# K's 32-point product of a long convolution: 64 by 64 quarters of the array in place of 128-row products

## The chip, the cores and the metric

The kernel runs on one core of one Trainium2 chip. The metric is the device time of one execution in microseconds, as the median of several runs.

## The reference

The block is a conditioned residual layer with two branches over 2048 positions and 576 channels:

```python
mod = (_silu(c) @ w_mod).reshape(c.shape[0], 6, 1, -1)
sa, ca, ga, sb, cb, gb = ...
h = _layernorm(x) * (1 + ca) + sa
x = x + ga * _A_ref(h, ...)      # state-space layer as a long convolution
h = _layernorm(x) * (1 + cb) + sb
x = x + gb * _B_ref(h, ...)      # gMLP with a 2048 x 2048 spatial product
```

In the first branch each channel d has a kernel of 2048 points, made of 128 complex poles, and is convolved with it:

```python
P = jnp.exp(logdA[:, :, None] * l[None, None, :])
K = jnp.einsum("dn,dnl,dn->dl", Cc, P, dB).real
y = irfft(rfft(up) * rfft(Kp))[..., :L] + u * Dskip
```

## The kernel before

The convolution is done by transforms written as matrix products, and the work of this document lies in its first part, where K is made and transformed. A point l of K is split into 32 steps of 64, l = 64 a + b. The 576 channels are taken in 36 groups of 16. For one group g, these functions run in order (lines of the profile):

- `e_unit` (L440 to 452) makes exponents on TensorE, into a tile of two PSUM banks (`ps2`, tile "ps") and one of a single bank (`ps1`, tile "pk"), and ScalarE takes the exponential.
- `t_unit` (L456 to 483) makes phases on TensorE into a "ps" tile. ScalarE (L480) and VectorE (L481) both read it.
- `s_unit` (L485 to 488) takes sine and cosine on ScalarE, `p_unit` (L490 to 502) multiplies on VectorE.
- `kg_unit` (L504 to 514) sums over the 128 poles: fp32 products with 32 columns of weights, four of them side by side in the array, into a "pk" tile. ScalarE copies it to the tile `kab`, whose 128 partitions are four channels by 32 points a, with 4 x 64 values on each.
- `d_unit` (L516) adds Dskip at one point.
- `k1_unit` (L520 to 535) is the 32-point product: for each of the four parts i of `kab` (128 partitions by 64 columns, the weights) and for the real and imaginary table `r1` (128 by 128, four equal 32 x 32 blocks on its diagonal, nothing elsewhere) one fp32 product of 64 output partitions by 128 columns, into one "pk" bank. The copy out of PSUM goes into the tile `k1t` on ScalarE (L535), or on VectorE (L533) for odd groups above nine.

The rest of the convolution goes by chunks of 128 channels: `u_unit` (L574, products L578) transforms the input, `z_unit` (L584, products L590, VectorE L591) finishes K's transform out of `k1t` and multiplies, `v_unit` (L594, products L598 and L599) goes back, `y_unit` (L637, products L644, VectorE L646) ends it and adds x. Between them results go out to HBM and back.

**PSUM.** There are eight banks. `ps2` hands out two tiles of two banks each, `ps1` four tiles of one bank each (L182 to 186). A tile is handed on when its last reader is done.

**What sets the order.** Groups 0 to 8 are written out by hand in a string (L725), beside the layer norm (`ln_half`, L423, whose products L431 take two "ps" tiles at a time) and the modulation (`mod_unit`, L342, products L349 and L354, two "ps" tiles each). From there on there are ticks 9 to 39 (L735). In a tick each letter of one of three strings calls a unit: t for group g, s for g-1, p for g-2, k and d for g-3 and 1 (that is `k1_unit`) for g-4:

```python
for n in ('kpt1svyzdeeu', 'ktespy1dzvu', 'ktvsdzuyp1')[tick % 3]:
```

This is the order in the code. TensorE, VectorE and ScalarE aren't tied to it in this stage: the framework lists each engine's instructions when the program is built, in the order of the code as long as its own estimate of the times lets the next one start, and with a later one ahead where the estimate says that the next one has to wait, for a PSUM tile for instance. On the chip the list is fixed. TensorE has one list for all these units, and each engine works through its own in order.

After the convolution the gMLP runs (from about 430 us to the end); most of its instructions are recorded under a helper's line, L152.

Of the kernel before, what the change touches and what calls it, by code (L numbers as in the profile page):

```python
# [164 lines left out]
def ssm(tc, I, x1_d, consts_s, dram, mod_d, mlp):  # L165
    nc = tc.nc
    V, A, G, T, S = nc.vector, nc.scalar, nc.gpsimd, nc.tensor, nc.sync
# [3 lines left out]
    with ExitStack() as ctx:  # L171
# [13 lines left out]
        def ps1():  # L185
            return psp.tile([128, 512], F32, name="pk", bufs=4)
# [3 lines left out]
        r1 = [small[:, 0], small[:, 1]]  # L190
# [4 lines left out]
        dsk = tb.tile([128, 144], F32, name="dsk", bufs=1)  # L195
# [241 lines left out]
        k1t = {}  # L437
# [66 lines left out]
        def kg_unit(g):  # L504
            pr, pi, gr, gi = tt.pop(g)
            pm = ps1()
            for i in range(4):
                for x_, y_, st in ((gr, pr, True), (gi, pi, False)):
                    for j in range(4):
                        c = 4 * i + j  # L510
                        T.matmul(pm[32 * j:32 * j + 32, 64 * i:64 * i + 64], x_[:, c], y_[:, c].rearrange("p s j -> p (s j)"),
                                 start=st, stop=not st, skip_group_check=True)
            kk = kab[g] = tb.tile([128, 4, 64], F32, name="kab")
            A.activation(kk, pm[:, :256].rearrange("p (i b) -> p i b", i=4), AF.Copy)
# [5 lines left out]
        def k1_unit(g):  # L520
            c, gi = divmod(g, 8)
            if gi == 0:
                k1t[c] = kp.tile([128, 32, 128], F32, name="k1")
            kk = kab.pop(g)
            pm = ps1()
            for i in range(4):
                for ri in range(2):
                    T.matmul(pm[64 * ri:64 * ri + 64, 128 * i:128 * i + 128], kk[:, i], r1[ri], start=True, stop=True,
                             skip_group_check=True)
            o = k1t[c][:, :, 16 * gi:16 * gi + 16].rearrange("p k (i j) -> p k i j", i=4)  # L530
            pk = pm.rearrange("p (i j k) -> p k i j", i=4, j=4)
            if g > 9 and g % 2:
                V.tensor_copy(o, pk)  # L533
            else:
                A.activation(o, pk, AF.Copy)  # L535
# [136 lines left out]
        V, T = mlp.tied.vector, mlp.tied.tensor  # L672

        def early_steps(order):
            nonlocal V, T, p0, p1
            pair = {}
            for s in order.split():
# [16 lines left out]
                elif n == "l":  # L694
                    S.dma_start(sel, I["c_sel"])
                elif n == "m":
                    q.dma_start(small, I["c_small"][:, 128:].rearrange("p (i c) -> p i c", i=6))
                elif n == "r":
                    r1_load(g, q)
                elif n == "a":  # L700
                    S.dma_start(msk, I["c_msk"])
                elif n == "b":
                    S.dma_start(dsk, I["dsk"])
                elif n == "I":
                    mod_init()
                elif n == "Q":
                    poles_load(g, mlp.tied.gpsimd)
                elif n == "M":
                    mod_unit(g)
                elif n == "S":  # L710
                    ln_stats(g)
                elif n == "V":
                    V = nc.vector
                elif n == "T":
                    T = nc.tensor
                elif n == "R":
                    pair[g] = ln_rows(2 * g), ln_rows(2 * g + 1)
                elif n in "AB":
                    ln_half(2 * g, pair[g], "AB".index(n))
                elif n == "C":  # L720
                    early.close()
                else:
                    {"e": e_unit, "t": t_unit, "s": s_unit, "p": p_unit, "k": kg_unit, "1": k1_unit, "d": d_unit}[n](g)
# [7 lines left out]
        wpre = ctx.enter_context(tc.tile_pool(name="wpre", reuse_waits="tile", bufs=2, side="right"))  # L731
        exps = iter(range(9, NG))
        lagged = {"t": (t_unit, 0), "s": (s_unit, 1), "p": (p_unit, 2), "k": (kg_unit, 3), "d": (d_unit, 3), "1": (k1_unit, 4)}
        passed = {"z": z_unit, "v": v_unit, "u": u_unit, "y": y_unit}
        for tick in range(9, NG + 4):  # L735
# [34 lines left out]
        V, A, G, T, S = mlp.nc.vector, mlp.nc.scalar, mlp.nc.gpsimd, mlp.nc.tensor, mlp.nc.sync  # L770
# [1374 lines left out]
def layout(inputs):  # L2145
    f = {k: np.asarray(v) for k, v in inputs.items()}

    def tok(a):
        g = a.reshape((32, 4, 16) + a.shape[1:])
        g = np.concatenate([g[:, 1::-1, ::-1], g[:, 2:]], axis=1)[:, [2, 3, 0, 1]]  # L2150
        return g

    out = {}
    x = f["A_u"][0]
    out["x"] = np.ascontiguousarray(tok(x).transpose(1, 0, 2, 3).reshape(128, 16, D))
    def pole(a):
        return np.ascontiguousarray(a.reshape(4, 9, 16, NST).transpose(0, 2, 1, 3).reshape(-1))

    for n in ("A_re", "A_im", "B_re", "B_im", "C_re", "C_im"):
        out["A_" + n] = pole(f["A_" + n])  # L2160
    out["A_log_dt"] = pole(np.repeat(f["A_log_dt"], NST))
    dsk = np.zeros((4, 32, 36, 4), f["A_Dskip"].dtype)
    dsk[:, 0] = f["A_Dskip"].reshape(36, 4, 4).transpose(2, 0, 1)
    out["dsk"] = dsk.reshape(128, 144)
    out["c"] = np.ascontiguousarray(f["c"].reshape(6, 96).T)
    out["w_mod"] = np.ascontiguousarray(f["w_mod"].reshape(6, 96, 6, 2, 288).transpose(1, 2, 3, 0, 4))
    out["w_in"] = f["B_w_in"]
    w = tok(f["B_w_sp"]).transpose(2, 1, 0, 3).reshape(L, L)
    w = tok(np.ascontiguousarray(w.T)).transpose(2, 1, 0, 3).reshape(L, L)
    out["w_spT"] = np.ascontiguousarray(w)  # L2170
    out["b_sp"] = np.ascontiguousarray(tok(f["B_b_sp"][:, None]).transpose(2, 1, 0, 3).reshape(L))
    out["w_out"] = f["B_w_out"]
    return out
# [24 lines left out]
```

## Time and profile before

| what | us |
|---|---|
| median of three runs | 1748.3 (1747.56 to 1751.75) |
| span of the profiled execution | 1749.5 |
| granted TensorE clock, mean | 0.982 |
| 1152 records of L511 (real part), one | 0.219, of which many overlap |
| 36 copies of L514, 128 x 256, one | 0.393 |
| 35 ScalarE sines of L487, 128 x 1024, one | 1.154 |
| 36 VectorE products of L499, 128 x 1024, one | 1.221 |

The page gives the profiled execution by its span, from the first to the last instruction; a time of its own beside the span isn't listed, so the sum is made against 1749.5 us and carried to the median, 1.2 us lower. An fp32 product shows as two records. A matmul's record lasts from its start to a modelled end, and records overlap in the array: how long TensorE is taken is read from start to start, not from the length of one. PEld is the weight load. In a row `x16` is the number of records merged into it. A row of the chain shows start, length, engine, tile and line.

### The profile page before, as it was taken

How to read it: one execution, taken by the hardware profiler on the slowest of the kernel's cores; microseconds unless marked ns; L12 is line 12 of the kernel's file. 1: busy time of each engine (PE TensorE's matmuls, PEld its weight loads, DVE VectorE, ACT ScalarE, POOL GpSimd, SP SyncE). 2: the span in 40 equal slices, each digit the busy share in tenths (PEclk: the TensorE clock that was granted, in tenths of full speed). 3: DMA queues.
4: the chain of work that ended last, by engine and by line, in shares of the span. 5: the costliest groups of instructions: out<-in, count | busy, mean ns of one | idle time of the engine just before them, and what ended most of it. 6: DMA issues, size and time to landing. Idle time of an engine off the chain costs nothing.

```text
span 1749.5 us, 36390 instructions
## 1 busy us (share of the span) xinstructions
PE 1654.4 (95%) x15174; PEld 1241.1 (71%) x15174; DVE 1256.1 (72%) x2259; ACT 834.3 (48%) x1121; POOL 250.5 (14%) x412
## 2 busy tenths in 40 slices
PE   2788999996999999999999999999999999999999
PEld 1344666664455446777878888888888888888887
DVE  7876999948999997888898767797444387334432
ACT  6877999834677665445443433343221233122210
POOL 4421332342122110000000000000111100111100
PEclk9897999998999999999999999999999999999999
DMA  8477656798698798777656887764766563556531
GB/s 227 136 223 229 187 155 170 207 271 248 215 292 272 222 249 290 258 253 261 221 193 205 289 290 263 241 231 138 246 219 231 195 224 106 194 197 208 193 110 41
DMA packets 182934, 376.24 MB, mean 215 GB/s; under 512 B 39105, under 2 KB 102977, under 8 KB 182001
## 3 DMA queue, kind: packets, MB, share of 16 engines
q1 hardware_dynamic: 138304, 168.50, 31.9%
q0 software_dynamic: 37984, 178.55, 31.2%
q10 hardware_dynamic: 6480, 26.86, 3.8%
q8 instruction: 119, 1.95, 0.5%
q14 instruction: 47, 0.38, 0.1%
HBM read 263.11 MB, written 101.31 MB: 208 GB/s over the span
## 4 chain that ended last, share of the span: by engine, by line
PE 32%; issue 28%; DVE 18%; DMA 4%; POOL 3%; ACT 2%; SPq 0%; POOLq 0%; ACTq 0%; DVEq 0%
PE ps L152 28%; POOL zset L1906 2%; DMA zset<-set_d 2%; DVE bsz L152 2%; DVE zset L152 1%; DVE n L152 1%; DVE gt L152 1%; DVE rq L152 1%; DVE wsp L152 1%; PE pk L578 1%; PE pk L598 1%; PE pk L590 1%; DVE pg L499 1%; DVE wso L152 1%; DVE ft L481 1%
## 5 line engine op out<-in xcount | busy, mean ns | idle before, releaser
L152 PEld LDWEIGHTS <-zset 128*128 128x128 f16 x7182 | 701.9, 98 | 92.6 <-DVE zset L152 7.6
L152 PE MATMUL ps<-wsp,zset 128*128 128x256 f16 x6048 | 667.7, 273 | 7.2 <-DVE zset L152 5.8
L152 PE MATMUL pz<-wz,nt 128*128 128x512 f16 (+1 forms) x1120 | 221.9, 358 | 9.0 <-DVE nt L152 4.3
L152 ACT ACTIVATE z<-gt 128x1024 f16<-128x1024 f32 x56 | 59.0, 1054 | 287.0 <-DVE gt L152 287.0
L152 PEld LDWEIGHTS <-nt 128*128 128x128 f16 x1120 | 109.1, 98 | 115.7 <-DVE nt L152 5.8
L1906 POOL DMA_DIRECT2D zset<-set_d x96 | 50.8, 529 | 869.1 <-PE ps L152 619.7
L152 DVE SCALAR_TENSOR_TENSOR gt<-ps,sc,bsp 128x512 f32<-128x512 f32 x36 | 27.0, 750 | 205.5 <-PE ps L152 203.8
L152 PE MATMUL ps<-wout,z 128*128 128x288 f16 x1344 | 170.0, 286 | 0.0
L152 PEld LDWEIGHTS <-z 128*128 128x128 f16 x1344 | 131.5, 98 | 33.0
L152 PE MATMUL ps<-n2o,zset 128*128 128x256 f16 x1134 | 128.2, 273 | 0.0
L152 DVE SCALAR_TENSOR_TENSOR gt<-ps,sc,gt 128x512 f32<-128x512 f32 (+1 forms) x180 | 122.2, 696 | 7.6
L152 DVE TENSOR_TENSOR raw<-raw 128x512 f32<-128x512 f32 (+2 forms) x228 | 119.2, 528 | 11.2 <-DMA raw<-z_d 6.9
L152 ACT ACTIVATE zset<-raw 128x1792 f16<-128x1792 f32 x48 | 81.2, 1691 | 58.3 <-PE ps L152 25.3
L152 DVE TENSOR_TENSOR zset<-raw,zset 128x1792 f16<-128x1792 f32 x48 | 97.0, 2020 | 15.9 <-ACT zset L152 15.9
L152 DVE TENSOR_TENSOR z<-ps,z 128x512 f32<-128x512 f32 (+1 forms) x126 | 72.0, 599 | 36.8 <-ACT z L152 26.7
L152 ACT ACTIVATE wsp<-raw,sc 128x1792 f16<-128x1792 f32 x25 | 44.6, 1785 | 42.7 <-DVE raw L152 35.0
L152 ACT ACTIVATE z<-z,sc 128x1024 f32<-128x1024 f32 x21 | 24.1, 1148 | 75.6 <-DVE z L152 71.9
L152 ACT ACTIVATE z<-pz,sc 128x512 f32<-128x512 f32 (+1 forms) x96 | 52.0, 582 | 16.2 <-DMA z_d<-z 9.8
L152 PE MATMUL ps<-n2q,wf 128*128 128x512 f16 x252 | 55.7, 379 | 0.0
L152 ACT ACTIVATE z<-z,nm,r 128x1152 f32<-128x1152 f32 x24 | 31.5, 1342 | 49.7 <-DVE nm L152 29.3
L152 PE MATMUL ps<-wout,z1b 128*128 128x288 f16 x384 | 52.6, 286 | 0.5 <-ACT z1b L152 0.5
L152 DVE SCALAR_TENSOR_TENSOR wsp<-raw,sc,wsp 128x1792 f16<-128x1792 f32 x25 | 51.9, 2078 | 0.0
(345 smaller groups left out, 2452.7 us busy)
## 6 DMA issues: line engine op xcount, KB each, us to landing
zset<-set_d POOLq DMA_DIRECT2D x96, 896.0 KB, 4.9
raw<-z_d SPq DMA_DIRECT2D x48, 512.0 KB, 5.5
set_d<-zset ACTq DMA_DIRECT2D x24, 896.0 KB, 5.9
z_d<-z POOLq DMA_DIRECT2D x32, 576.0 KB, 9.7
zset<-wa_d POOLq DMA_DIRECT2D x18, 896.0 KB, 4.9
raw<-in_w_spT SPq DMA_DIRECT2D x25, 512.0 KB, 4.4
set_d<-zset SPq DMA_DIRECT2D x12, 896.0 KB, 5.5
u_d<-st1o POOLq DMA_DIRECT2D x16, 576.0 KB, 4.8
```

What stands on the lines that cost most here:

```text
L152: return self.tc.keep_in_program_order(f(*a, **k))
L481: V.scalar_tensor_tensor(f, f, MAGIC, pa, op0=ALU.subtract, op1=ALU.subtract)
L499: V.tensor_tensor(pr, pi, c3[:, :, None, :].to_broadcast([128, 16, 2, 32]), op=ALU.mult)
L578: T.matmul(pm, fwd, u1, start=True, stop=True)
L590: T.matmul(pm[:, w * j:w * j + w], cst[k // 8][:, k % 8], k1t[c][:, k, :w], start=True, stop=True)
L598: T.matmul(pm, inva, zz[:, 0], start=True, stop=False)
L1906: self.nc.gpsimd.dma_start(o, self.set_d[f, j - 1] if j else self.wa_d[f])
```

## The change

The table `r1` is block diagonal, so the products of rows 0 to 63 with columns 64 to 127, and the other way round, are all zero. The change leaves these out: it takes the two halves of 64 rows apart, with weights `kk[s, i]` (64 partitions by 64 columns), moving table `r1[ri][s, s]` (64 by 64). Row half h and output half ri choose one of four quarters of the array. A group has 16 products in place of 8, each with 64 moving columns in place of 128. The two row halves write to two banks, so the result lies in a "ps" tile of two banks (half of each is used) in place of a "pk" tile of one. So that the 16 channels of a group still come out in order, `kg_unit` puts them into `kab` in another order, and Dskip is laid out on the host to match.

```diff
             for i in range(4):
                 for x_, y_, st in ((gr, pr, True), (gi, pi, False)):
                     for j in range(4):
-                        c = 4 * i + j
+                        c = 8 * (j // 2) + 2 * i + j % 2
                         T.matmul(pm[32 * j:32 * j + 32, 64 * i:64 * i + 64], x_[:, c], ...)
...
             kk = kab.pop(g)
-            pm = ps1()
+            pm = ps2()
             for i in range(4):
                 for ri in range(2):
-                    T.matmul(pm[64 * ri:64 * ri + 64, 128 * i:128 * i + 128], kk[:, i], r1[ri], start=True, stop=True,
-                             skip_group_check=True)
-            o = k1t[c][:, :, 16 * gi:16 * gi + 16].rearrange("p k (i j) -> p k i j", i=4)
-            pk = pm.rearrange("p (i j k) -> p k i j", i=4, j=4)
+                    for h in range(2):
+                        s = slice(64 * h, 64 * h + 64)
+                        T.matmul(pm[64 * ri:64 * ri + 64, h, 64 * i:64 * i + 64], kk[s, i], r1[ri][s, s], start=True, stop=True,
+                                 skip_group_check=True)
+            o = k1t[c][:, :, 16 * gi:16 * gi + 16].rearrange("p k (h c) -> p k h c", h=2)
+            pk = pm[:, :, :256].rearrange("p h (c k) -> p k h c", c=8)
             if g > 9 and g % 2:
                 V.tensor_copy(o, pk)
             else:
...
-    dsk[:, 0] = f["A_Dskip"].reshape(36, 4, 4).transpose(2, 0, 1)
+    dsk[:, 0] = f["A_Dskip"].reshape(36, 2, 4, 2).transpose(1, 3, 0, 2).reshape(4, 36, 4)
```

## The prediction

> **What bounds the kernel now.** I read the page first, for the share of each engine in the whole span.
>
> ```profile
> PE 1654.4 (95%) x15174; PEld 1241.1 (71%) x15174; DVE 1256.1 (72%) x2259; ACT 834.3 (48%) x1121; POOL 250.5 (14%) x412
> ```
>
> TensorE is busy nearly all the time, but most of that belongs to the gMLP behind the convolution, which this change doesn't touch. So I asked for the busy time of each engine by stage of the convolution. The columns are window, PE, PEld, DVE, ACT, POOL (us and instructions), granted clock, DMA share, GB/s.
>
> ```profile
> 50.00:180.00 130.00, 103.43 (x1531) 56.47 (x1528) 96.96 (x191) 101.84 (x150) 37.20 (x57) 0.82 0.64 197
> 180.00:320.00 140.00, 137.46 (x2095) 85.72 (x2094) 135.62 (x170) 134.71 (x181) 45.48 (x79) 1.00 0.61 170
> 320.00:380.00 60.00, 59.56 (x677) 37.70 (x676) 40.52 (x52) 33.10 (x49) 21.83 (x40) 1.00 0.81 228
> 380.00:430.00 50.00, 36.12 (x273) 25.38 (x273) 34.80 (x89) 22.66 (x25) 14.88 (x21) 0.86 0.98 282
> ```
>
> There are three different limits. From 50 to 180 us no engine is full. From 180 to 320 us three engines are full at once: PE idles 2.5 us of 140, DVE 4.4, ACT 5.3. From 320 to 380 us only PE is full. The chain of work that ended last (start, length, what) confirms the last two.
>
> ```profile
> by line: DVE pg L498 12.4%; DVE pg L499 11.9%; DVE ft L481 11.6%; DVE zz L591 9.9%; issue 7.8%; DVE ft L482 7.5%; DVE et L501 5.9%; PE pk L578 4.1%; DVE et L500 3.9%; DMA v_d<-v 3.8%; DVE xb L646 3.4%; PE pk L511 3.0%; DVE k L533 3.0%; PE p
> ...
> 209.58 1.02 PE pk L528 x16
> 210.60 1.03 PE pk L511 x64
> ...
> 295.97 0.90 PE pk L528 x16
> ...
> 330.92 1.02 PE pk L528 x16
> ...
> 340.63 1.02 PE pk L644 x16
> 341.65 0.87 PE pk L528 x16
> ...
> 343.57 1.02 PE pk L528 x16
> ...
> 352.06 0.87 PE pk L528 x16
> ...
> 369.26 1.75 PE pk L528 x32
> ...
> 399.95 5.32 DMA v_d<-uu
> ```
>
> The first line is the chain from 250 to 320 us: mostly DVE. From 326 us on the chain is PE almost without a break. The stage ends in a few DMA round trips (the last row) that start from PE's end, so a shift there moves everything behind it. How many of the 36 units (16 records each) lie in each stage comes from the line's own view.
>
> ```profile
> L528 PE MATMUL pk<-small,kab x160: 272/273/476, 70.6 to 179.3; 128*64 128x128 f32 x160
> L528 PE MATMUL pk<-small,kab x98: 272/273/323, 319.8 to 370.7; 128*64 128x128 f32 x98
> ```
>
> 160 records are ten units before 180 us; 98 are six units (and two records of the one before) after 320; twenty lie between.
>
> **The change part by part: the product itself.** Today a unit is 8 products, each two records. Two units back to back take 1.75 us for 32 records, 54.7 ns each, although one record lasts 273 ns (row above): two column halves overlap. A unit behind one of the same shape takes 0.87 us (341.65, behind L644's 128*64), and 1.02 us behind another shape, so a change of shape costs about 0.15 us. After the change a unit is 16 products, 32 records, each of 64 rows by 64 columns with 64 moving columns. The trace has no such record. Its nearest row is L511: also fp32 with 64 moving columns, in four column strips, 64 records in 1.03 us; less 0.15 us that is 13.8 ns each. Whether strips of rows overlap as well is shown by L431, fp32, 32 rows by 64 columns.
>
> ```profile
> 111.40 0.33 PE L431 MATMUL ps<-gsp,cs 32*64 32x288 bf16 x4
> 111.53 0.69 PE L431 MATMUL ps<-ln_x,rt 32*64 32x288 f32 x8
> 112.15 0.65 PE L528 MATMUL pk<-small,kab 128*64 128x128 f32 x6
> ```
>
> Its eight fp32 records give way to the next after 0.62 us, 78 ns each. One such record without overlap would need 288/64 of L511's 4 x 13.8 = 55 ns, that is 248 ns; so four row strips run at once, each into a bank of its own. I therefore take 32 x 13.8 = 0.44 us, with a change of shape 0.59 us, against 1.02: 0.43 us gained per unit, and 0.28 us where the unit stood behind L644, since that is now another shape too. The bounds: if only two of the four quarters overlap, 27.6 ns a record, 0.88 us, there is no gain; a loss (55 ns, 1.77 us) would need no overlap at all, which today's column halves exclude; all 36 units at 0.43 us would be 15.5 us.
>
> The Trainium skill speaks against this in "TensorE: Matmul & The Clock Gate", section "Wait — 56ns, not 53.3ns?": from start to start a matmul never takes less than about 25 ns, however short. By that a unit would take 32 x 25 = 0.80 us and the gain would be 0.07 us. L511's 13.8 ns over 64 records does not agree, and the row decides.
>
> **Where that gain lands.** In the PE-bound tail: 1.02 + 0.87 + 1.02 + 0.87 + 1.75 = 5.53 us today. After: four at 0.59 and the pair at 64 x 13.8 + 0.15 = 1.03, together 3.39. That is **2.1 us** at the end of the chain. Between 180 and 320 us the chain passes through four units (the first and the last are shown), three at 1.02 and one at 0.90: **1.6 us**. It can't be much more there: DVE alone has 135.6 us of work in 140, so 4.4 us is the ceiling, and behind PE it is DVE that is late next. Before 180 us PE is idle a fifth of the time, and I count nothing. Sum: 3.7 us earlier.
>
> **The copies, and what costs nothing.** Line 514, 518, the order of the products on L511 and the layout of dsk only rename columns: the same instructions, 36 of each. The copies out of PSUM read 512 elements as before, from two banks instead of one.
>
> ```profile
> L535 ACT ACTIVATE k<-pk 128x512 f32<-128x512 f32 x23 | 13.8, 602 | 1.9 <-PE pk L528 1.8
> L433 ACT ACTIVATE st1o<-ps 128x576 f32<-128x576 f32 x32 | 19.8, 651 | 16.9 <-PE ps L431 11.9 <-DMA u_d<-st1o 2.6 <-ACT gar L371 1.0
> L533 DVE COPY k<-pk 128x512 f32<-128x512 f32 x13 | 8.9, 687 | 1.3 <-PE pk L528 1.2
> ```
>
> L433 reads 576 elements from two banks in 651 ns, 1.13 ns each; L535 reads from one at 1.18. So two banks cost nothing on ACT, and I take the same for DVE. A twentieth either way on 36 copies of 0.6 to 0.7 us would be 1.1 us. No DMA and no queue is moved.
>
> **The wait that is added.** This is the part that decides. The result moves from the pool of four single banks ("pk") to the pool of two double banks ("ps"), which the phases (L465 to L481) and the exponentials (L448, L449) use already, one of each per tick. A third tile must find one of the two free. Between 180 and 335 us there are seven places where today's order starts L528 while both are held; the first and the last:
>
> ```profile
> 197.85 0.28 PE L465 MATMUL ps<-sel,lc 48*128 48x256 bf16 x2
> ...
> 198.29 0.39 PE L448 MATMUL ps<-sel,lb 48*128 48x512 bf16 x2
> ...
> 198.94 1.09 PE L528 MATMUL pk<-small,kab 128*64 128x128 f32 x16
> ...
> 200.33 1.08 ACT L449 ACTIVATE et<-ps 128x1024 f32<-128x1024 f32 x1
> 200.53 1.22 DVE L481 SCALAR_TENSOR_TENSOR ft<-ft,ps 128x1024 f32<-128x1024 f32 x1
> ...
> 330.71 1.04 ACT L449 ACTIVATE et<-ps 128x1024 f32<-128x1024 f32 x1
> ...
> 330.85 1.09 PE L528 MATMUL pk<-small,kab 128*64 128x128 f32 x16
> ```
>
> At 198.94 both tiles are taken; the first comes free when L449 ends, at 201.41, so L528 would wait 2.5 us. At 330.85 it is 0.9 us. The seven come to 13.2 us. On PE the products of z, v and u stand behind it, and ACT and DVE wait for those. That is the upper bound, if PE simply stands still. The lower bound is nothing, if the planner that lists PE's instructions puts the ready products of z and v ahead of the waiting unit. That it does so is shown by a case of today: in the code both exponentials of a tick come before u.
>
> ```profile
> 235.95 0.39 PE L448 MATMUL ps<-sel,lb 48*128 48x512 bf16 x2
> ...
> 236.72 1.02 PE L578 MATMUL pk<-u,small 128*128 128x512 f32 x2
> 237.67 0.39 PE L448 MATMUL ps<-sel,lb 48*128 48x512 bf16 x2
> ```
>
> Here u (L578) went ahead of the second one. I take three tenths of the 13.2 us, **4.0 us**, nearer to nothing since the planner sees such waits, but not nothing, since a list made in advance can't follow the actual times and a k1 that is late holds "ps" longer for the next phases. The pool "pk" gets a user less; PE's 2.5 us of idle time are the ceiling of that, and I count none.
>
> Before 180 us "ps" carries the layer norm and modulation products too, and PE already waits for it:
>
> ```profile
> PE ps L469 <- ACT et L449: 3.1, 1, 3.1
> ...
> PE ps L448 <- ACT et L449: 2.9, 1, 2.9
> ...
> PE ps L431 <- DVE ft L477: 2.7, 3, 2.0
> ...
> PE ps L448 <- ACT st1o L433: 2.5, 2, 2.3
> PE ps L469 <- ACT st1o L433: 2.4, 1, 2.4
> ...
> PE ps L431 <- ACT st1o L433: 1.9, 3, 1.1
> ```
>
> These six are 15.5 us over some 62 tiles (32 of L431, 12 of the modulation, nine each of phases and exponentials), 0.25 us each. Ten more tiles make 2.5 us; with PE idle a fifth of the time I take half, **1.2 us**.
>
> Sum: -3.7 + 4.0 + 1.2 = +1.5 us. The profiled execution's span is 1749.5 us, 1.2 us over the median of the three runs and inside their range, so on the median the forecast is 1748.3 + 1.5 = **1749.8 us**: gain and new waits nearly cancel.
>
> **The rivals.** *The cover is complete.* The planner hides every wait, and the third engine's slack is used up: 2.1 us in the tail and the whole 4.4 us of DVE, 6.5 us, 1741.8 us. For it: z and v are ready in time, and DVE can't lose by the change. Against: it asks all of DVE's idle time, and today's chain gives 1.6.
>
> *The pool is the bound (slower).* PE's list stays as it is at most of the seven places, and each k1 tile that is copied late by a busy ACT or DVE also delays the next phase. With all 13.2 us and 2.5 us early, less 3.7: +12 us, 1760.3 us. It decides from the point where two thirds of the waits stay uncovered (8.8 + 1.2 - 3.7 = 6.3 us). For it: both readers are over 96% busy, so release is slow; against: the swap of L578 and L448.
>
> *The quarters don't overlap in four.* Then a unit costs 0.88 us as today, the gain is nothing, and the waits remain: +5.2 us, 1753.5 us. Against it: L511 and L431. The rule of the Trainium skill that stands above ("TensorE: Matmul & The Clock Gate") would come to nearly the same.
>
> **How the numbers follow.** A measurement of this kernel can tell about 0.3%, 5.2 us, from no change. The forecast has 0.40, complete cover 0.24, the pool as the bound 0.28, no overlap 0.08 (half of it beyond 5.2 us; the other half counts as within, and some of the forecast's own spread lies beyond). So faster by over 0.3%: 0.24; within: 0.40; slower: 0.36. The forecast's own range, with waits from 0 to two thirds, is 1744.6 to 1754.6. The range for 8 in 10 reaches to both sides' prices: 1741.5 to 1760.0.
>
> **What would show it.** In the profile after, L528 has 1152 records of 64*64; a unit in the chain near 350 us should be 0.44 to 0.6 us long, and near 0.9 if the quarters don't overlap. PE's waits for ps before L528, with L449, L481, L533 or L535 as releaser, should add up to a few us, and L590 or L598 should stand ahead of L528 where today it follows L451. The busy time of L533 and L535 should stay. What would make the prediction wrong is a list that the planner orders anew over the whole stage, so that the other engines' order moves too: no row of today shows that.

## The result, and the profile after

The changed kernel takes 1765.4 us (median of four, 1761.6 to 1766.4), the kernel before, run beside it, 1750.0 us (1747.6 to 1753.9). The ratio is 1.0078, with an interval of 1.0058 to 1.0098: **slower by about 14 us**, where 1749.8 us was forecast, and beyond the upper end of the range (1760.0).

The profiled execution has a span of 1759.9 us (its time is 1761.6), 10.4 us more than the one before. The engines' busy time shows nothing of that: TensorE has 5 us less to do than before, and the other engines the same as before within 1.4 us.

```profile
PE 1649.4 (94%) x15750; PEld 1232.0 (70%) x15750; DVE 1256.3 (71%) x2259; ACT 835.7 (47%) x1121; POOL 250.2 (14%) x412
```

The three stages are the same windows as before; the columns are again window, PE, PEld, DVE, ACT, POOL, granted clock, DMA share, GB/s.

```profile
50.00:180.00 130.00, 98.30 (x1579) 51.65 (x1579) 88.24 (x181) 93.30 (x139) 35.27 (x54) 0.78 0.58 177
180.00:320.00 140.00, 126.48 (x2305) 75.82 (x2305) 133.68 (x168) 134.03 (x179) 42.93 (x75) 1.00 0.60 171
320.00:380.00 60.00, 57.54 (x901) 34.89 (x903) 45.64 (x59) 39.34 (x57) 20.79 (x38) 1.00 0.72 209
```

Before 180 us every engine does less in the same 130 us: DVE 88.2 for 97.0, ACT 93.3 for 101.8. Work has been pushed out of this window. In the ticks PE has fallen from 137.5 to 126.5, DVE by 1.9 and ACT by 0.7 only. In the tail PE is nearly full again.

What the change promised is there. In the chain of the changed kernel, a unit (now 32 records) and a pair of units (64) read:

```profile
344.31 0.62 PE ps L530 x32
...
352.04 0.62 PE ps L530 x32
...
353.69 0.62 PE ps L530 x32
...
362.70 0.62 PE ps L530 x32
...
379.64 1.09 PE ps L530 x64
```

The forecast was 0.59 and 1.03 us. The quarters do work side by side, and 5.53 us of the tail's chain are now 4 x 0.62 + 1.09 = 3.57, a gain of 1.96 us where 2.1 was forecast. The copies cost what they cost before (the page's groups: busy time, mean ns of one, idle time ahead of them):

```profile
L537 ACT ACTIVATE k<-ps 128x512 f32<-128x512 f32 x23 | 13.7, 595 | 3.9 <-PE ps L530 3.9
```

```profile
L535 DVE COPY k<-ps 128x512 f32<-128x512 f32 x13 | 8.9, 682 | 0.4 <-PE ps L530 0.4
```

595 and 682 ns stand against 602 and 687.

To find where the time went, I follow one instruction that every group has once, the end of its phases on VectorE (L482), in all kernels. First its rows for groups 4 to 10 (seven instructions), before and after, then those for groups 27 to 34 (eight):

```profile
L482 DVE TENSOR_SCALAR ft<-ft x7: 693/694/695, 89.6 to 159.5; 128x1024 int32<-128x1024 int32 x7
```

```profile
L482 DVE TENSOR_SCALAR ft<-ft x7: 686/693/695, 90.6 to 168.4; 128x1024 int32<-128x1024 int32 x7
```

```profile
L482 DVE TENSOR_SCALAR ft<-ft x8: 681/686/694, 280.6 to 331.9; 128x1024 int32<-128x1024 int32 x8
```

```profile
L482 DVE TENSOR_SCALAR ft<-ft x8: 679/682/693, 288.1 to 345.1; 128x1024 int32<-128x1024 int32 x8
```

So **early** (groups 4 to 10) takes 69.9 us before and 77.8 after; the **ticks** (10 to 27) 121.1 and 119.7; **late** (27 to 34) 51.3 and 57.0; the **tail** (group 34 to the last product of z on VectorE) 61.8 and 58.3. That is +7.9, -1.4, +5.7 and -3.5 us; with 1.0 us ahead of group 4 and 0.7 behind the stage it makes the 10.4 us of the spans. Two places lose, and neither is where the prediction put most of its waits (the ticks). These four lengths serve as the measure of every experiment:

| kernel | early | ticks | late | tail | ratio to before (interval) |
|---|---|---|---|---|---|
| before | 69.9 | 121.1 | 51.3 | 61.8 | |
| after | 77.8 | 119.7 | 57.0 | 58.3 | 1.0078 (1.0058 to 1.0098) |
| e1 pool alone | 79.0 | 119.4 | 52.3 | 60.7 | 1.0062 (1.0044 to 1.0080) |
| e2 groups 0 to 9 | 77.7 | 119.9 | 55.0 | 60.8 | 1.0084 (1.0066 to 1.0102) |
| e3 groups 10 to 35 | 68.9 | 120.4 | 57.9 | 58.4 | 1.0042 (1.0028 to 1.0057) |
| e4 groups 30 to 35 | 67.1 | 119.3 | 52.4 | 60.0 | 0.9995 (0.9982 to 1.0009) |
| e5 letters moved | 78.8 | 119.7 | 56.9 | 58.3 | 1.0078 (1.0056 to 1.0100) |
| e6 two single banks | 71.1 | 124.1 | 61.5 | 59.3 | 1.0091 (1.0074 to 1.0108) |
| e7 only the letters | 72.2 | 119.3 | 51.3 | 61.8 | 1.0043 (1.0024 to 1.0061) |
| e8 L499 kept | 78.5 | 119.7 | 57.2 | 59.4 | 1.0069 (1.0054 to 1.0085) |
| e9 groups 23 to 29 old | 78.7 | 119.7 | 52.6 | 61.0 | 1.0041 (1.0026 to 1.0056) |
| e10 banks early, quarters last | 71.1 | 121.6 | 52.4 | 59.3 | 1.0019 (1.0006 to 1.0032) |
| e11 sines kept | 81.7 | 119.7 | 52.7 | 59.4 | 1.0053 (1.0037 to 1.0070) |
| e12 as e3, sines kept | 70.1 | 119.8 | 52.7 | 59.4 | 1.0002 (0.9989 to 1.0015) |

The lengths come from one profiled execution each. Single executions of one kernel lie up to some 10 us apart, part of it behind the stage, where the lists of all these kernels are the same; so the ratios come from the medians, and the lengths say where. How far the early length moves by itself is seen in four kernels whose ScalarE and VectorE have the same lists up to 187 us: 69.9 in the kernel before, 68.9 in e3, 67.1 in e4, 70.1 in e12.

### The profile page after: what moved, and what is told of

Its sections match the earlier page's. It is cut to its first block, busy times and chain, and to the rows that moved or that the text cites. A ratio compares the mean times of both kernels' runs of the same rounds, so it can differ in the third digit from the quotient of the medians.

```text
span 1759.9 us, 37536 instructions
## 1 busy us (share of the span) xinstructions
PE 1649.4 (94%) x15750; PEld 1232.0 (70%) x15750; DVE 1256.3 (71%) x2259; ACT 835.7 (47%) x1121; POOL 250.2 (14%) x412
## 4 chain that ended last, share of the span: by engine, by line
PE 60%; DVE 15%; DMA 4%; issue 3%; ACT 2%; POOL 0%; SPq 0%; ACTq 0%; DVEq 0%; POOLq 0%
PE ps L152 56%; DVE bsz L152 2%; DMA zset<-set_d 2%; DVE zset L152 1%; DVE n L152 1%; DVE rq L152 1%; DVE wsp L152 1%; DVE gt L152 1%; DVE wso L152 1%; DMA wst<-in_w_in 1%; ACT z L152 1%; PE pk L600 1%; PE pk L580 1%; DVE z L152 1%; PE pk L592 1%
## 5 line engine op out<-in xcount | busy, mean ns | idle before, releaser
L499 DVE TENSOR_TENSOR pg<-et,ft 128x1024 f32<-128x1024 f32 x36 | 43.8, 1218 | 13.6 <-ACT ft L487 10.9
L152 PE MATMUL ps<-wout,z1b 128*128 128x288 f16 x384 | 52.4, 286 | 0.0
```

Source lines behind the costliest of these rows:

```text
L152: return self.tc.keep_in_program_order(f(*a, **k))
L499: V.tensor_tensor(pr, pi, c3[:, :, None, :].to_broadcast([128, 16, 2, 32]), op=ALU.mult)
```

## The experiments

**e1: the pool without the quarters.** The kernel before, with only the tile taken elsewhere:

```diff
-            pm = ps1()
+            pm = ps2()[:, 0]
```

> The products stay as before (128 rows, 128 columns), only the result lies in one bank of a double tile of the pool ps. If the pool is the cause, the loss of the change plus the gain of the quarters must show: 13 us lost by the change and 4 to 6 us gained by shorter products make 15 to 20 us slower than before. If the quarters or their new list of instructions are the cause, this is within 3 us of before.

Measured: 1762.65 us, 1.0062. The pool alone makes most of the loss, 11 us by the ratio, less than the pool theory's 15 to 20 and far from nothing. Its early part is that of the changed kernel (79.0 us), its late part is not (52.3). The row of its first k1 products shows what the pool does first: they begin at 98.6 us, as in the changed kernel, where the kernel before has 70.6.

```profile
L528 PE MATMUL ps<-small,kab x144: 272/273/476, 98.6 to 179.2; 128*64 128x128 f32 x144
```

**e2, e3, e4: the change for some groups only.** The condition chooses between the two forms of `k1_unit`, and with it the order of the products on L511 and of dsk. The cut is of e2; e3 has `g > 9` in its place and e4 `g > 29`.

```diff
-            pm = ps1()
...
+            if g < 10:
+                pm = ps2()
...
+            else:
+                pm = ps1()
...
```

> The change for groups 0 to 9 alone, those whose product ran before 180 us; groups 10 to 35 as before. If the loss is made in the part that is ordered by hand, where the layer norm and the modulation take the same double tiles, 8 to 11 us slower than before. If it is made by the ticks, within 3 us of before.

> The change for groups 10 to 35 alone. If the loss is made in the early part, between 4 us faster and 3 us slower than before: 2 us gained at the PE-bound end, the waits of the ticks against the gain there. If the waits in the ticks are the cause, 8 to 13 us slower.

> The change for groups 30 to 35 alone, whose products stood on the PE-bound end of the stage, where phases and exponentials need few tiles any more. If the terms for the quarters are right, 1.5 to 2.5 us faster than before. If a new list of instructions costs in itself, slower by some us.

Measured: 1765.47, 1758.12 and 1749.29 us. e2 is slower than expected, e3 lies between its two expectations, e4 gains 0.9 us by the ratio where 1.5 to 2.5 were expected, which is within the noise. The table sorts it: e2 has the early loss (77.7) and e3 doesn't (68.9), e3 has the late loss (57.9). So the two losses are separate. One thing didn't fit at the time: e2's late part is 55.0 us, 3.7 longer than before, although none of its groups behind 9 was changed.

**e5, e7: k1 earlier in the hand-written string.** In the string k1 stands behind the layer norm and the modulation, which use ps too. One theory was that it now starts late because of that place. The changed kernel around its first units:

```profile
97.46 1.24 PE L354 MATMUL ps<-mpart,small 128*128 128x288 f32 x4 [0.75 <-ACT mpart L351]
...
98.63 1.50 PE L530 MATMUL ps<-small,kab 64*64 64x64 f32 x64
...
98.74 0.65 ACT L371 ACTIVATE gar<-ps 128x576 f32<-128x576 f32 x1 [1.33 <-PE ps L354]
...
99.39 0.60 ACT L537 ACTIVATE k<-ps 128x512 f32<-128x512 f32 x1
```

Both units of groups 0 and 1 come right behind the modulation (L354), and the second needs its copy (L371) first. So I moved the letters, in the change (e5) and in the kernel before as a control (e7):

```diff
-... r2 d0 w3 e5 ... p3 d1 r3 R3 M3 10 11 s4 ... d2 12 S3 ... d3 B4 ... r7 13 d4 t7 ... d5 14 C
+... r2 d0 10 w3 e5 ... p3 d1 11 r3 R3 M3 s4 ... d2 12 S3 ... d3 13 B4 ... r7 d4 14 t7 ... d5 C
```

> The whole change, with one further edit: in the string that orders the early part by hand, the letters of k1's first five groups stand right behind the groups' d (10 to 14 behind d0 to d4), where the profile of the changed kernel has them 0 to 28 us later than the kernel before had them (98.6 for 70.6 us in group 0, 157.4 for 128.2 us in group 4). Theory of the place: a product that takes a tile of the pool ps gets it in the order of the code, so it stands behind the layer norm's and the modulation's tiles, and that is what the early part loses. Then k1 of groups 0 to 4 starts near the kernel before's times again (within 8 us of them), the phases of group 10 (L482) start within 3 us of the kernel before in place of 8.9 us later, and the time falls by 6 to 10 us from the changed kernel's 1765.5: 1755 to 1760. Theory of the occupancy: ten more users of a pool of two tiles cost what they cost wherever they stand, since every one of them waits for a copy and holds up the next user. Then the phases of group 10 are still 5 us or more late, and the time is 1761 to 1767.

> The kernel before, with only the early letters moved as in e5_early_moved (10 to 14 behind d0 to d4): the control for that edit. Since k1 there takes a tile of pk and started up to 28 us ahead of its place already, both theories expect no change: 1748 to 1754, the phases of group 10 within 2 us of the kernel before. Were it 3 us or more faster or slower, that amount belongs to the edit and not to the pool, and e5 is read against it.

Measured: e5 1763.56 us, e7 1757.94. The k1 of groups 0 to 4 did start earlier (77.5 for 98.6 us in group 0, 138.9 for 157.4 in group 4), and yet early takes 78.8 us. The control lost 7.5 us by the ratio, which neither theory expected; 2.3 of them are in its early part, the rest isn't located (ScalarE's and VectorE's lists are the kernel before's again behind 156 us). e5's time lies in the range of the theory of occupancy, but its own expectation says that it has to be read against the control when that moves by 3 us or more. Against e7, e5 still loses 6.6 us of early length where the changed kernel loses 7.9 against the kernel before, but by the ratios only 6 us where the changed kernel loses 13.7. So **the place alone isn't the cause of the early loss**; that it has a part in it isn't ruled out.

**e6: quarters without ps.** Each row half writes a pk tile of its own and is copied by itself.

```diff
-            pm = ps2()
+            pms = [ps1(), ps1()]
...
-                        T.matmul(pm[64 * ri:64 * ri + 64, h, 64 * i:64 * i + 64], kk[s, i], r1[ri][s, s], ...)
+                        T.matmul(pms[h][64 * ri:64 * ri + 64, 64 * i:64 * i + 64], kk[s, i], r1[ri][s, s], ...)
...
+            for h, pm in enumerate(pms):
+                o = k1t[c][:, :, 16 * gi + 8 * h:16 * gi + 8 * h + 8]
+                pk = pm[:, :256].rearrange("p (c k) -> p k c", c=8)
```

> The quarters of the change, but out of the pool pk: each half of the rows writes a single-bank tile of its own, and each tile is copied out by itself (256 elements of each partition a copy, in place of one copy of 512). Theory of the pool: what was lost before 168 us was the pool ps. Then k1 of group 0 starts at 70 to 75 us again, the phases of group 10 are within 3 us of the kernel before, the tail limited by TensorE keeps its gain of 2 to 4 us, and the second copy costs ACT and DVE an estimated 0.2 us in each group (two of 0.386 us as at L514 against 0.60 us at L535: 36 x 0.17 = 6 us of work, a third of it on the path, 2 us): 1747 to 1753. Theory of the rival that two of pk's four tiles are too many for the ticks, where the kernel products, z, v, u and y take them as well: the early part recovers, but the ticks from 180 to 345 us lose 5 to 10 us: 1754 to 1762. Theory that the quarters themselves (32 records with their loads, not the pool) cost the early part: the phases of group 10 are again 5 us or more late.

Measured: 1766.85 us. The early part is back (71.1 us, k1 from 69.2 us on), with all the quarters in place, so, together with e1, **the early loss is the pool and not the quarters**.

```profile
L530 PE MATMUL pk<-small,kab x320: 218/218/366, 69.2 to 177.2; 64*64 64x64 f32 x160
```

The ticks and the late part lose 13.2 us against the changed kernel's 4.3 (124.1 + 61.5, and 119.7 + 57.0, against 172.4), more than the rival's 5 to 10. How much of that is pk's tiles and how much the doubled copies isn't separated.

**e8: VectorE's list.** In the late part VectorE's list differs from the one before: L499 of the groups 27 and 33 stands ahead of the tick's phases. I kept these two in place (the framework's tie to program order).

```diff
-            V.tensor_tensor(pr, pi, ...)
+            (mlp.tied.vector if g in (27, 33) else V).tensor_tensor(pr, pi, ...)
```

> The whole change, with VectorE's product L499 of the groups 27 and 33 alone kept at its place in the order of the code. In the list of the changed kernel these two stand ahead of the phases of the tick (L481, L482), in the kernel before and in e1_pool_only they stand behind them; the products and their ps tiles stay as in the change. Theory of the list: the 4 to 5 us lost between 288 and 345 us (the phases of groups 28, 30 and 34) come from VectorE waiting in places where the new list has a product of the next group ahead. Then the wait of L499 for L511 of 2.6 us goes, the phases of group 34 (L482) start 8 to 10 us later than in the kernel before in place of 13.2, the end of the stage is 5 to 8 us later in place of 9.7, and the time falls by 2 to 5 us to 1760 to 1763.5. Theory of the pool: these 4 to 5 us are waits for the tiles of ps, whatever VectorE's list is. Then group 34 is still 12 to 14 us late and the time 1764 to 1767.

Measured: 1764.65 us, late 57.2. The wait of L499 for L511 is gone, but L481 waits for ScalarE in its place, 3.8 us for 0.2. The longest wait of VectorE from 282 to 358 us (total, times, longest) in the changed kernel, and in e8:

```profile
DVE pg L499 <- PE pk L511: 2.6, 1, 2.6
```

```profile
DVE ft L481 <- ACT ft L480: 3.8, 1, 3.8
```

**VectorE's list isn't the cause**; VectorE waits for something that is late on ScalarE.

**e9: the old product for groups 23 to 29.** These are the groups whose k1 falls into the late part. The cut is against the kernel before; the change holds for the other groups, with the order on L511 and dsk to match.

```diff
-            pm = ps1()
...
+            if g < 23 or g > 29:
+                pm = ps2()
...
+            else:
+                pm = ps1()
...
```

> The change for groups 0 to 22 and 30 to 35, the old product (128 rows, one bank of pk) for groups 23 to 29, whose products fall between about 270 and 330 us. The early loss stays as it is: the phases of group 20 are 6 to 8 us later than in the kernel before. Theory that the late loss comes with the list that these groups get: VectorE's list is the kernel before's again from tick 28 to tick 31, the phases of group 34 are 6 to 9 us late in place of 13.2, the end of the stage 4 to 6 us in place of 9.7, the time 1758 to 1762. Theory that the early loss alone matters and the rest is regained anyway before the end: the end of the stage stays 9 to 10 us later, 1764 to 1767.

Measured: 1759.39 us, late 52.6: the late loss is gone, as the theory of the list had it, though these groups took no ps tile either, so e9 alone can't tell the list from the pool. The early loss is 8.8 us in this execution, so the end of the stage is 9.8 us late all the same, and of the tail's gain 0.8 us is left.

**e11: ScalarE's list.** The exponentials and sines stand in ScalarE's list too, and here is what the changed kernel does at the first late tick:

```profile
288.86 1.15 ACT L487 ACTIVATE ft<-ft,consts_s 128x1024 f32<-128x1024 f32 x1 [2.04 <-DVE ft L482]
290.03 1.28 ACT L449 ACT_TABLE_LOAD   x1
291.32 1.02 ACT L449 ACTIVATE et<-ps 128x1024 f32<-128x1024 f32 x1
...
294.10 0.63 ACT L581 ACTIVATE uu<-pk 128x512 f32<-128x512 f32 x1
294.58 0.43 ACT L514 ACTIVATE kab<-pk 128x256 f32<-128x256 f32 x1
294.84 1.16 ACT L480 ACTIVATE ft<-ps,consts_s 128x1024 f32<-128x1024 f32 x1
```

The first sine of group 27 (L487) stands ahead of the exponentials. It waits 2.04 us for VectorE's L482 of the same group, and the four exponentials, the copies of u and `kab` and the phases of the next group (L480) come after it. In e1 the same list has this sine behind the next phases, and the exponentials follow v at once:

```profile
287.07 0.59 ACT L600 ACTIVATE v<-pk 128x512 f32<-128x512 f32 x1
287.68 1.28 ACT L449 ACT_TABLE_LOAD   x1
289.17 1.02 ACT L449 ACTIVATE et<-ps 128x1024 f32<-128x1024 f32 x1 [0.21 <-PE ps L448]
```

Group 33 shows the same, with 2.03 us. So the whole change, with the sines of these two groups kept in place:

```diff
-            A.activation(ct, ct, AF.Sin, bias=halfpi, scale=-TWO_PI)
-            A.activation(f, f, AF.Sin, scale=-TWO_PI)
+            (mlp.tied.scalar if g in (27, 33) else A).activation(ct, ct, AF.Sin, bias=halfpi, scale=-TWO_PI)
+            (mlp.tied.scalar if g in (27, 33) else A).activation(f, f, AF.Sin, scale=-TWO_PI)
```

> The whole change, with the sines of the groups 27 and 33 (L487 and L488) kept at their place in the order of the code. In the changed kernel's list for ScalarE the first sine of these two groups stands ahead of the four exponentials of the tick: there ScalarE waits 2.04 and 2.03 us for VectorE (L482), and the exponentials, u's and kab's copies and the next phases (L480) come that much later; in the kernel before and in e1_pool_only it stands behind them. With the two kept, both engines' lists from there on are those of e1_pool_only. Theory of ScalarE's list, in place of VectorE's, which e8 ruled out: the loss of 4 to 5 us from 288 to 345 us is these waits. Then the phases of group 34 (L482) are 7 to 10 us late in place of 13.2, about what group 27 is, the end of the stage is 4 to 7 us late in place of 9.7, and the time is 1759 to 1762. Theory of the pool: the loss is k1's tiles of ps in these ticks, which this edit leaves as they are: group 34 is 12 to 14 us late, the time 1764 to 1767.

Measured: 1761.11 us, 1.0053 for 1.0078, which is 4.4 us. Late takes 52.7 us for 57.0, with every product and every tile of ps as in the change, and ScalarE's waits for L482 in this stretch fall from 5.6 us (four times) to 1.9. The first row is of the changed kernel, the second of e11:

```profile
ACT ft L487 <- DVE ft L482: 5.6, 4, 2.0
```

```profile
ACT ft L487 <- DVE ft L482: 1.9, 2, 1.0
```

VectorE's list in e11 is e8's, and TensorE's the changed kernel's, each but for a few neighbours that change places; what separates e8's 57.2 us from e11's 52.7 is above all where ScalarE takes the sines. So **the late loss is ScalarE's list**. By its time the expectation of the list holds; by the moment of group 34 (13 us late) it does not, since in this execution the early part was 3.9 us longer than the changed kernel's, with the same lists up to there. Its late part is still 1.4 us longer than the kernel before's; e1, e4, e9, e10 and e12 have 1.0 to 1.4 us of that too. Most of it is a shift of the boundary at group 34, given back in the tail: late and tail together take 113.1 us before, 113.0 in e1, 113.6 in e9, 112.4 in e4 and 112.1 in e11 and e12.

The same kind of slip stands in e2. Its late groups are the old ones, but its list puts a sine of group 33 between the copies of u and the next phases, with two loads of the function table (1.28 us each) that the kernel before doesn't have:

```profile
334.68 1.28 ACT L487 ACT_TABLE_LOAD   x1
335.97 1.15 ACT L487 ACTIVATE ft<-ft,consts_s 128x1024 f32<-128x1024 f32 x1
337.03 0.36 ACT L514 ACTIVATE kab<-pk 128x256 f32<-128x256 f32 x1
337.29 1.11 ACT L480 ACTIVATE ft<-ps,consts_s 128x1024 f32<-128x1024 f32 x1
338.41 1.28 ACT L449 ACT_TABLE_LOAD   x1
```

VectorE's longest wait for a sine in this stretch is 2.8 us, in e1 1.1. That this makes up the 3.7 us is argued; no run kept that sine in place. But a list that is made anew can differ over a hundred microseconds behind the edit.

**e10, e12: is there a version that gains?** e10 takes e6's form for groups 0 to 9, the old product for 10 to 29 and the change for 30 to 35. e12 is e3 with the edit of e11.

The cut is of e10.

```diff
+            if g < 10:
+                pms = [ps1(), ps1()]
...
+            if g > 29:
+                pm = ps2()
...
+            else:
+                pm = ps1()
...
```

> Quarters where nothing so far lost time by them: groups 0 to 9 with two single banks of pk and two copies as in e6_two_single_banks, groups 10 to 29 the old product, groups 30 to 35 the quarters of the change in a tile of ps as in e4_last_groups. Theory that the pool and the list are all that costs: the phases of group 10 are within 2 us of the kernel before, group 30 within 2 us, the end of the stage 1 to 4 us earlier, 1745 to 1750, within noise of e4_last_groups (1749.3) or up to 3 us better. Rival: with the copies doubled in the early part (two of an estimated 0.39 us in place of one of 0.60) and another list, 2 to 5 us are lost again before 200 us and 1752 to 1756 results.

> The same two groups' sines kept in place, with the change made for groups 10 to 35 only and the old product for groups 0 to 9 (e3_later_groups with the edit of e11). Theory that the early pool and ScalarE's list are all that costs, and the quarters gain in the tail: the phases of group 30 are 1 to 3 us earlier than in the kernel before, the end of the stage 2 to 6 us earlier in place of 1.4 later, the time 1745 to 1750 (e3_later_groups: 1758.1). Theory that the ps tiles of groups 10 to 35 cost by themselves: 1754 to 1759.

Measured: 1754.65 (1.0019) and 1752.79 us (1.0002, interval 0.9989 to 1.0015). e10 misses its first expectation; its early part is the old one within 1.2 us, its ticks take 121.6 us where e4 and e7, with the list of the kernel before there, take 119.3; why, and whether that is the 3.3 us by the ratio, isn't settled. e12 is e3 without its loss: 7 us by the ratio from the order of two groups' sines. Its first ten k1 units take no ps tile, the other 26 do, and it is as fast as the kernel before; its expectation of 1745 to 1750 was too good. None of the kernels is faster than the kernel before by more than the noise; the best is e4.

## Why the prediction was wrong, by its steps

**The product: right.** 0.62 us a unit and 1.09 a pair, against 0.59 and 1.03. From one unit to two it is (1.09 - 0.62) / 32 = 14.7 ns a record; L511's 13.8 ns was the right row. The Trainium skill ("TensorE: Matmul & The Clock Gate", "Wait — 56ns, not 53.3ns?") has a floor of about 25 ns from start to start; 14.7 ns does not agree, as L511 had said.

**The tail: the products right, what arrives less.** 2.1 us were forecast, and the rows of the chain give 1.96. But the 3.5 us by which the tail is shorter are in part the shifted boundary. From group 27 to the last product of z, e4 gains 0.7 us, e11 and e12 1.0. The forecast let the whole gain through. In the kernel before TensorE waits for nothing from 330 to 390 us; in e4, with the quarters of the last groups alone, it waits 0.5 us for VectorE's product of z and 0.4 us for a transfer of u. Behind a faster TensorE the next waits come up.

**The copies: right.** Two banks cost no more than one.

**The gain of 1.6 us in the ticks: not there.** With nothing changed between the groups 10 and 27, e4 and e7 take 119.3 us there; the changed kernel takes 119.7. The 1.4 us by which it is below the kernel before's profile belong to that execution of the kernel before.

**The waits for ps in the ticks, 4.0 us: they are there, but nothing is paid for them.** From 180 to 290 us TensorE waits 5.5 us before its k1 units, each time for the copy of an earlier k1:

```profile
PE ps L530 <- ACT k L537: 3.2, 3, 1.3
PE ps L530 <- DVE k L535: 2.3, 2, 1.4
```

Yet the groups 10 to 27 take 119.7 us, 119.4 in e1 with the tiles of ps and the old products, and 119.3 in e4 and e7 without either. TensorE had become shorter there (busy 126.5 us of 140 in place of 137.5), while VectorE and ScalarE stayed nearly full: the saved work and the waits are both TensorE's, and neither reaches the time. In places the list also put the ready products ahead, as the prediction argued. At the tick where the kernel before has L528 at 330.85 us (a row of the prediction) with L590 and L598 behind it, the changed kernel has z and v first:

```profile
341.54 1.06 PE L592 MATMUL pk<-k,cst 128*128 128x128 f32 x8
...
342.43 1.02 PE L600 MATMUL pk<-zz,small 128*128 128x512 f32 x2
...
344.24 0.69 PE L530 MATMUL ps<-small,kab 64*64 64x64 f32 x32
```

What was paid in the late part, 4.3 us of the 5.7, is not the tiles of ps: e1 takes them and doesn't have the loss, e11 takes them, and the quarters, and doesn't have it either. It is ScalarE's list. The prediction named this among what would make it wrong (that the planner orders the list anew over the whole stage) and gave it no price.

**The early part, 1.2 us: the step that failed.** The sentence was: "Ten more tiles make 2.5 us; with PE idle a fifth of the time I take half". Measured: the seven kernels whose groups 0 to 9 use ps take 77.7 to 81.7 us from group 4 to 10, 78.9 in the mean; the seven others 67.1 to 72.2, 70.1 in the mean. The pool costs **8.8 us** here, seven times the term. By the ratios, e11 and e12, which differ in the groups 0 to 9 alone, are 8.9 us apart, the changed kernel and e3 6.3. The term took the mean wait of today's tiles as the price of another one. But a tile more is a tile held: the unit at 157.44 us holds one until its copy ends 1.80 us later.

```profile
157.44 1.13 PE L530 MATMUL ps<-small,kab 64*64 64x64 f32 x32
...
158.64 0.60 ACT L537 ACTIVATE k<-ps 128x512 f32<-128x512 f32 x1 [0.80 <-PE ps L530]
159.13 0.38 ACT L514 ACTIVATE kab<-pk 128x256 f32<-128x256 f32 x1
...
160.32 1.13 PE L530 MATMUL ps<-small,kab 64*64 64x64 f32 x32
...
161.52 0.60 ACT L537 ACTIVATE k<-ps 128x512 f32<-128x512 f32 x1 [2.01 <-PE ps L530]
162.01 0.38 ACT L514 ACTIVATE kab<-pk 128x256 f32<-128x256 f32 x1
```

At 98.63 it is 1.36 us. Ten tiles at 1.4 to 1.8 us, with two to share them, are 7 to 9 us if somebody always waits for one. That fits 8.8, but it is arithmetic, and no run tried it (a third ps tile, for instance). The waits don't bear it out as the whole: from 50 us to group 10 TensorE's waits before products into ps (without L354's for its own data) come to 20.7 us in the mean of the seven kernels and 17.5 in the others (e7, whose early part is 72.2 us, has 21.6), so some 3 us of the 8.8 are seen there. The same rows show a second thing: each copy into `kab` comes 1.7 us behind the start of a k1. `kab` has two buffers, so group 6 can't have one before group 4's k1 has read its own: 159.13 us here, 143.10 before. In all seven kernels that lose, the copy of a group's `kab` (groups 2 to 8) starts 1.3 to 4.7 us behind the start of the k1 of the group two before it; in the seven others it is 6.9 us or more. That this is the way in which the loss spreads to the next groups fits all fourteen, but no run gave `kab` a third buffer, so it is argued, not shown. And "PE idle a fifth of the time" was no cover, by the measured 8.8 us; that the idle time lies in gaps between things that wait for each other, ps among them, is the likely reason.

The Trainium skill has the rule that would have pointed there: "TensorEngine Tiling (Array Packing)", section "Gotcha 1: PSUM Pressure", says that tiles of rows need a PSUM bank each and that this raises the pressure on PSUM. The runs agree that the pool decides, and give it a size here: the same product costs 11 us more through a tile of the two-bank pool without any tiling of rows (e1).

**The rivals.** The pool as the bound, on the slower side with 0.28, gave 1760.3 us: nearest, and right that the pool decides, but it put its price of 13.2 us into the ticks, where nothing was paid. Complete cover was right that no wait is paid in the ticks, and wrong about the 4.4 us that it gained there. That the quarters don't overlap is refuted.

**The sum by the lengths:** 8.8 for the early part, 0.4 for the ticks, 4.3 for ScalarE's list, less 1.0 for late and tail, are 12.5 us against 13.7 by the ratio (10.2 to 17.2), where the forecast had 1.2, 2.4, nothing and -2.1.

**What stays open:** how the 8.8 us divide between the tiles, `kab` and the clock (next but one section); and that the kernel before loses 7.5 us by five letters (e7).

## What to carry to other kernels

A buffer taken from a busy pool isn't priced by the waits that the pool's users have today: the term made from them was seven times too small here. A better first estimate is the time for which the new user holds it, over the number of buffers; it came out right here, but no run tested it by itself. Ask also what the late result holds back in turn (here the two buffers of `kab`). A gain on one engine counts only until the next engine's wait, so check who waits once it is faster. And where a planner makes the engines' lists, an edit is paid for in the lists too, even far behind it: compare the order on every engine, not only the one that was edited, look at the engine that others wait for, and pin the instruction that has slipped.

## What the runs showed of the hardware

The quarters run four at a time: in the unit at 319.04 us four records start 6 to 7 ns apart, and the next four 38 to 39 ns after them, which makes the 14.7 ns a record.

The early loss comes with a lower clock. From group 4 to group 10 TensorE's granted clock is 0.71 to 0.81 in the seven kernels that lose there, and 0.83 to 0.90 in the seven others. Whether the waits lower the clock or the lower clock lengthens the waits, no run separates; the kernel before has a window at 0.50 too (140 to 150 us). In the changed kernel and in e6, with the quarters in both (windows of 10 us, columns as above):

```profile
140.00:150.00 10.00, 5.79 (x97) 2.76 (x88) 4.43 (x6) 8.57 (x12) 1.75 (x3) 0.85 0.52 180
150.00:160.00 10.00, 9.24 (x156) 5.10 (x152) 6.87 (x10) 5.46 (x8) 2.02 (x3) 0.50 0.45 159
160.00:170.00 10.00, 8.24 (x115) 3.99 (x115) 4.00 (x5) 8.42 (x11) 0.00 (x0) 0.50 1.05 325
```

```profile
140.00:150.00 10.00, 7.49 (x144) 3.92 (x141) 5.71 (x7) 6.77 (x10) 2.26 (x3) 0.83 0.42 151
150.00:160.00 10.00, 8.46 (x190) 5.02 (x184) 7.37 (x10) 9.25 (x15) 0.75 (x1) 1.00 0.94 300
160.00:170.00 10.00, 6.66 (x190) 4.46 (x178) 8.12 (x10) 9.99 (x18) 2.24 (x4) 1.00 0.88 272
```

In the changed kernel TensorE is busy 5.8 us of 10 from 140 to 150, and then runs at half clock for 20 us: its records last longer, so it looks busier than in e6 (9.24 us for 156 records, 8.46 for 190). A high busy share at a clock of 0.50 is less work, not more. The Trainium skill ("TensorE: Matmul & The Clock Gate", "HAM oscillation — how this bites in real kernels") ties the halved clock to gaps of TensorE of more than about 3.4 us. The trace doesn't agree: the 4.2 us of idle time ahead of the drop are several gaps, and the longest between two matmul records from 125 to 160 us is 2.19 us (145.14 to 147.32). A gap of 2.21 us in e6 (160.91 to 163.12) left the clock at 1.00, so the longest gap alone doesn't decide it here. The clock moves between executions: the early part of e11 and of the changed kernel, with the same lists, differ by 3.9 us, at 0.71 and 0.77.
